# When the mixer runs: fixed stretches in place of a budget, and mirror blocks queued behind the last x

## The chip, the cores and the metric

The kernel runs on one core of one Trainium2 chip. The time is the device time of one execution in microseconds (us); the figure that counts is the median of the runs, and less is better.

## What is computed

For each of 8 batches there are 3008 rows of 256 channels (u, v) and of 64 channels (z). An attention without softmax gives x, and a token and channel mixer follows:

```python
scores = (1 / S) * (z @ z.T)
x = u * ((np.maximum(scores, 0.0) ** 2) @ v)
h = np.maximum(x.T @ w_tok1, 0.0) @ w_tok2        # over rows: 3008 -> 256 -> 3008
y = x + h.T
out = y + np.maximum(y @ w_ch1, 0.0) @ w_ch2      # over channels: 256 -> 1536 -> 256
```

## The kernel before, in words

**Tiles.** The rows of a batch make 6 column blocks q of 512 (the last has 448) and 6 key groups g of 512. Block (b, q) is the sum over all g of attention(g, q) times v(g), held transposed in two PSUM pairs, acc0 and acc1, one for each half of the channels. A score matmul (L424) contracts over 64 rows and uses half of TensorE's rows, and so does the attention product acc (L646), which is split into two 64-row halves. The two halves of a pair run side by side: this text calls that half mode. All products of the mixer use all 128 rows: full mode. Going from one to the other is a mode switch; the planner counts 0.095 us for it (`on_pe`).

**From scores to attention.** Each score pair goes through a relu on ScalarE (`relu`, L462; L450 for the diagonal) and a square on VectorE (`square`, L470; `square_triangle`, L499) into a buffer `at` (6 of them). The scores are symmetric, so block (b, q) for g > q is computed once and turned for block (b, g): `flip` (L515) issues a DMA transpose on SyncE's queue from `at` into a buffer `fl` (10 of them). These turned ones are the mirror blocks. The diagonal block ("triangle", q = g, from batch 2 on) is computed for its upper part alone, and three small DMA transposes in place (`flip_tiles`, L511) fill in the lower part before the product reads it.

**End of a block.** `finish` adds the two halves of acc (ScalarE copy L771, VectorE add L777), `gate` (L798) multiplies with the turned u and writes xT, and `turn_x` (L811) turns x by a DMA transpose on SyncE's queue.

**Mixer of a batch** (`add_mixer`). Two lists of pieces: heads are 6 token products `tok1` (L851, into a_ps), which need the last x of the batch, then 6 `tok2` (L870, into h_ps), whose result is added to xT; tails are for each block 6 channel products `ch1` (L911, into hp, relu on ScalarE L925 or VectorE L927 into h2pre) and 3 or 4 output tiles `ch2` (L955, into op), whose residual add (L971) needs another turned copy of xT (L893) and ends in a store (L976). One such list is worked off in its own order.

**Order of the work.** The order on every engine is fixed when the program is built, by a planner with its own costs. PSUM is a ring of bank pairs that scores, acc and mixer share. The main loop (from L1260) picks at each step a score unit, an attention step or a mixer piece. The mixer was let in by a budget: every attention or score step of batch 1 and later adds to it in proportion to its time, every mixer piece draws on it, and a stretch may begin only between blocks, from batch 1 on, before an even q. Loads (u, v, z) are software DMAs on GpSimd's queue, asked for at fixed steps of the block loop (`at_group`) and issued at least 4.5 us apart (`ask_some`), each behind a small copy (`mark`, L120) that ties it to finished work. SyncE's queue takes all transposes and all stores in program order, so an instruction that waits there holds up all behind it.

Of the kernel before, what the change touches and what calls it, by code (L numbers as in the profile page):

```python
# [44 lines left out]
class Piece:  # L45


    def __init__(self, cost, needs, fn, opens=False, closes=False, room=None,
                 urgent=False):
        self.cost, self.needs, self.fn = cost, needs, fn  # L50
        self.opens, self.closes, self.room = opens, closes, room
        self.urgent = urgent


@with_exitstack
def kernel(
# [12 lines left out]
    B, S, D = u.shape  # L69
# [398 lines left out]
    def square(unit, view, t):  # L468
        (b, q, g), pr = unit
        nc.vector.tensor_mul(view, view, view)  # L470
        if (b, q, g) in early:
            for e in early[b, q, g][2 * pr:2 * pr + 2]:
                e.t = t
            if pr == 0:
                blocks[b, q, g] = (
                    Done(t), ats[b, q, g].rearrange("p (i w) -> p i w", w=QW), "at", [1])
            else:
                ats.pop((b, q, g))
            return
        if pr < GK // 2 - 1:  # L480
            return
        at = ats.pop((b, q, g))
        uses = [1]
        if flips(b, q, g):
            uses[0] = 2
            attn = at.rearrange("p (j i s) -> p i j s", i=GK, s=P)
            done = push("sp", t, 1.8, 6.5, lambda t: flip(b, q, g, at, uses, done),
                        room=("fl",))
        else:
            attn = at.rearrange("p (i w) -> p i w", w=QW)  # L490
        blocks[b, q, g] = (Done(t), attn, "at", uses)
        recent[0] = at[:, :1]
# [212 lines left out]
    def do_half(start, g):  # L705
        blk = cur[0]
        if blk.whole:
            return do_whole(start, g)
        if blk.g is None:
            start_bundle(blk, g, start)  # L710
        g, dh, tiles = blk.steps[blk.half]
        blk.half += 1
        final = blk.slot == NG and not any(
            d == dh or d is None for _, d, _ in blk.steps[blk.half:])
        if dh is not None and blk.acc[dh] is None:
            blk.home[dh], free_at = take_slot()
            blk.acc[dh] = bank_pair(blk.home[dh], f"acc{dh}")
            start = max(start, free_at)
        start, end = on_pe(start, "half", len(tiles) * column_time(blk.W))
        for i in tiles:  # L720
            for h in range(2):
                av_matmul(blk, g, i, h if dh is None else dh, h, final and i == tiles[-1])
        if final:
            finish(blk, dh, end)
        if blk.half == len(blk.steps):
            blk.g = None
            for g in blk.bundle:
                _, _, name, uses = blocks.pop((blk.b, blk.q, g))
                release(name, uses, pe[0] + 0.2)
                used[blk.b, g] = used.get((blk.b, g), 0) + 1  # L730
                if blk.b == 0 and blk.q == NQ - 1:
                    live["fl"] -= 1
            if blk.slot == NG:
                end_block(blk)
# [52 lines left out]
    def gate(blk, dh, acc, t):  # L787
        b, q, W = blk.b, blk.q, blk.W
        uT = uTs[b, q]
        if dh == 0:  # L790
            xTs[b, q] = sb.tile([P, DT, QW], BF16, tag="xT", name="xT", bufs=ROOM["xT"])
            live["xT"] += 1
            live["x"] += 1
            if W < QW:
                nc.gpsimd.memset(xTs[b, q][:, :, W:], 0.0)
        xT = xTs[b, q]
        full, rest = W // P, W % P
        nc.vector.tensor_mul(  # L798
            xT[:, dh, :full * P].rearrange("p (t s) -> p t s", s=P),
            acc[:, :full * P].rearrange("p (t s) -> p t s", s=P),  # L800
            uT[:, :full, dh, :])
        if rest:
            nc.vector.tensor_mul(
                xT[:, dh, full * P:W], acc[:, full * P:W], uT[:, full, dh, :rest])
        if dh == DT - 1:
            gated[0] += 1
            push("sp", t, 1.25, 7.5, lambda t: turn_x(b, q, t), first=1)

    def turn_x(b, q, t):
        x = sb.tile([P, DT, QW // P, P], BF16, tag="x", name="x_sb", bufs=ROOM["x"])  # L810
# [23 lines left out]
    def add_mixer(b):  # L834
# [163 lines left out]

        for q in range(NQ):
            heads.append(Piece(0.874, [x_done[b, NQ - 1]], lambda end, q=q: tok1(q, end),  # L1000
                               opens=q < NQ - 1, closes=q > 0))
        for q in range(NQ):
            heads.append(Piece(4 * column_time(widths[q]), [a_done, tok2_done[q]],
                               lambda end, q=q: tok2(q, end)))
        def add_ch1(q, c2):
            h2_done[q, c2] = Done()
            tails.append(Piece(4 * column_time(widths[q]), [u_done[q]] + w_done[:2],
                               lambda end: ch1(q, c2, end),
                               room=("h2", "us") if c2 == 0 else ("h2",)))

        def halves(q):

# [10 lines left out]
        def add_ch2(q, half, i):  # L1023
            two = not alone(q, half)
            needs = [Sooner(h2_done[q, c2], 0.218 * c2) for c2 in range(CHT // 2)]
            tails.append(Piece(1.312, needs + w_done[2:],
                               lambda end: ch2(q, half, i, end), opens=two and i == 0,
                               closes=two and i == 1))


        early = ROOM["h2"] - CHT // 2
        for q in range(NQ):
            for c2 in range(early if q else 0, CHT // 2):
                add_ch1(q, c2)
            if q + 1 < NQ:
                for c2 in range(early):
                    add_ch1(q + 1, c2)
            for half in halves(q):
                for i in range(pieces_of(q, half)):
                    add_ch2(q, half, i)  # L1040

    def next_piece(t):

# [8 lines left out]
        for l in lists:  # L1052
            if not l:
                continue
            p = l[0]
            if p.opens and not p.closes and opened[0] is not None:
                continue
            r = max(t, known(*p.needs))
            if p.room and not has_room(p.room):
                r = FAR  # L1060
            if not p.closes:
                r = max(r, min(slots)) if slots else FAR
            if r < FAR and r <= t + 0.05:
                return r, l
            if r < best[0]:
                best = r, l
# [77 lines left out]
    for b in range(B):  # L1144
# [9 lines left out]
        if b + 1 < B:  # L1154
            at_group(base + NG, lambda b=b: new_zT(b + 1))
            for j, c in enumerate(vorder):
# [2 lines left out]
                    if j % 3 == 2:  # L1159
                        at_group(base + NG + j // 3 + 8, lambda b=b, j=j: turn_next_z(b, j // 3))  # L1160
                else:
                    at_group(base + 2 * NG + 2 + j,
                             lambda b=b, j=j: ask(lambda: z_then_turn(b + 1, j)))
                    at_group(base + (NQ - 1) * NG - 2 + (j if j > 1 else 0),
                             lambda b=b, c=c, j=j: ask(
# [61 lines left out]
    for k, item in enumerate(items):  # L1227
        at_group(NG + 1 + k * (NQ * NG - 2 * NG + W_LATER) // len(items), item)

    per_batch = 0.87 * NQ * (2 + CHT // 2) + 1.35 * 4 * NQ  # L1230
    flat = NQ * NG * 1.73 + NQ * (NQ + 1) / 2 * 0.44
    fill(7, bank_pair(0, "wp")[:, 0, :])

    for c in range(DT):
# [12 lines left out]
    late_z(5, 9.0)  # L1247
    first_u(18.5)

    done_units = 2  # L1250
    budget = 8.0
    NOW = 0.05
    STARVED = 0.7
    BACKLOG = 0.9
    GRAIN = 2
    SWING = 2.0
    SPACING = 4.5
    SLOW = 0.84
    LONG = 12.0
    while cur[0] is not None or heads or tails:  # L1260
        run_engines(pe[0])
        ask_some()
        t = pe[0]
        ta, g = next_half(t)
        tm, pieces = next_piece(t)
        blk = cur[0]

        def has_turned(us):
            return known(*(turned[b, c] for (b, q, g_), _ in us for c in (q, g_)))
# [30 lines left out]
        by_then = [s for d, s in ring if (guess.get(s, FAR) if d.t is None else d.t) <= need]  # L1300
        spare = need > t + 1.7 or len(by_then) > 1

        between = blk is None or blk.acc[0] is None
        mixer_now = tm <= t + NOW and (budget > -SWING or blk is None)
        pick = None

        together = (
            runs and blk.q > 1 and not blk.tails
            and blk.slot == 0 and t + 0.3 < tails_ready(blk) < FAR)
        if not runs:  # L1310
            if mode[0] == "full" and mixer_now:
                pick = "mixer"
            elif mode[0] == "half" and between and mixer_now and (
                    blk is None or blk.b > 0 and blk.q % 2 == 0):
                pick = "mixer"
            elif n_now and spare and queued < BACKLOG and ts <= t + NOW:
                pick = "scores"
            elif ta <= t + NOW:
                pick = "av"
            elif n_now and spare and ts <= t + NOW:  # L1320
                pick = "scores"
            elif mixer_now:
                pick = "mixer"
        elif n_now and not together and ts <= t + NOW and (whole or (low and n_now >= 2)):
            pick = "scores"
        elif (starved and now and can_score(done_units, now) == now
# [8 lines left out]
        elif ta <= t + NOW:  # L1335
            pick = "av"
        if pick is None:
            options = [(ta, "av"), (tm, "mixer")]
            if n_now and (whole or low if runs else spare):
                options.append((ts, "scores"))  # L1340
            when, what = min(options)
            op = next_op()
# [22 lines left out]
                for f in fetch.get(s, []):  # L1365
                    f()
        else:
            if not pieces[0].urgent:
                budget -= pieces[0].cost
            do_piece(tm, pieces)  # L1370
        if pick != "mixer" and blk is not None and blk.b >= 1:
            budget += per_batch * (pe[0] - t) / flat * (SLOW if blk.b == 1 else 1.0)
    run_engines(FAR)


# [28 lines left out]
```

## Time and profile before

| What | Value |
|---|---|
| median of 5 runs (lowest to highest) | 1147.67 us (1146.7 to 1148.45) |
| the profiled execution: its time, its span | 1148.45 us, 1146.7 us |
| TensorE matmuls | 9219 |
| VectorE, ScalarE, GpSimd busy | 56%, 48%, 13% |
| hardware DMA queue (transposes, stores), software DMA queue (loads): share of the 16 engines | 58.0%, 21.5% |

The span runs from the first to the last instruction. "L646" is line 646 of the kernel, "acc<-at,v_sb" reads: writes tile acc, reads tiles at and v_sb. SPq is SyncE's queue: the time shown there is that of issuing a DMA, and the landing is later. In a timeline equal instructions that follow each other are merged, with their count behind an x.

### The profile page before, as it was taken

To read this page: it belongs to the slowest core of one execution; us is meant where nothing else is said; L and a number is where in the kernel's file an instruction comes from. 1 tells how busy PE (TensorE), PEld (TensorE's weight loads), DVE (VectorE), ACT (ScalarE), POOL (GpSimd) and SP (SyncE) were. 2 spreads that over 40 slices of the span, in tenths; PEclk is the share of its full clock that TensorE was granted. 3 is DMA by queue.
4 is the path that set the end of the run, shared out by engine and by line. 5 is a ranking of instruction groups with operands and counts; after the bars stand their busy time and mean duration, and the time that the engine had idled before them with its cause. 6 is when DMAs were issued, how large, how long until landed. Compare 5 with 4: busy or idle time off the path is not lost.

```text
span 1146.7 us, 22470 instructions
## 1 busy us (share of the span) xinstructions
PE 1137.0 (99%) x9219; PEld 673.4 (59%) x9219; DVE 638.4 (56%) x947; ACT 549.3 (48%) x699; POOL 154.2 (13%) x387
## 2 busy tenths in 40 slices
PE   8999999999999999999999999999999999999998
PEld 3455465646557566565565655665566556566666
DVE  6887454565554755537545375554644656434544
ACT  7999534374342742526525354344543554422331
POOL 4500110200111001111111100111002110000000
PEclk9999999999999999999999999999999999999999
DMA  9999964985979868799588996799877998642121
GB/s 155 187 177 193 185 124 100 196 139 125 158 136 200 163 113 156 127 201 162 113 157 142 175 183 108 154 144 186 164 125 141 146 184 152 120 103 56 51 83 65
DMA packets 468199, 164.85 MB, mean 144 GB/s; under 512 B 431936, under 2 KB 445824, under 8 KB 468096
## 3 DMA queue, kind: packets, MB, share of 16 engines
q1 hardware_dynamic: 440240, 130.72, 58.0%
q0 software_dynamic: 27344, 32.32, 21.5%
q8 instruction: 72, 1.18, 0.4%
q10 hardware_dynamic: 512, 0.38, 0.1%
q14 instruction: 31, 0.25, 0.1%
HBM read 65.40 MB, written 24.64 MB: 79 GB/s over the span
## 4 chain that ended last, share of the span: by engine, by line
PE 97%; DMA 2%; DVE 0%; ACT 0%; SPq 0%; issue 0%; POOL 0%; ACTq 0%; DVEq 0%
PE acc L646 40%; PE op L955 21%; PE hp L911 21%; PE sc L424 6%; PE a_ps L851 4%; PE h_ps L870 4%; PE first_acc L563 1%; DMA zf<-in_z_dram 1%; DMA fl<-at 0%; DMA at<-at 0%; DMA v_sb<-in_v_dram 0%; DVE h2pre L927 0%; ACT at L462 0%; SPq L159 0%; PE up L1196 0%
## 5 line engine op out<-in xcount | busy, mean ns | idle before, releaser
L646 PEld LDWEIGHTS <-v_sb 64*128 64x128 bf16 x4418 | 239.5, 94 | 224.1 <-issue 6.5
L646 PE MATMUL acc<-at,v_sb 64*128 64x512 bf16 (+1 forms) x2738 | 341.8, 374 | 1.7 <-ACT at L462 1.3
L925 ACT ACTIVATE h2pre<-hp 128x1024 bf16<-128x1024 f32 (+1 forms) x161 | 160.8, 1000 | 315.0 <-PE hp L911 314.7
L462 ACT ACTIVATE at<-sc 128x1024 bf16<-128x1024 f32 (+1 forms) x294 | 288.0, 1027 | 33.8 <-PE sc L424 26.5
L911 PE MATMUL hp<-xT,w_ch_sb 128*128 128x512 bf16 (+1 forms) x1152 | 257.3, 375 | 0.0
L470 DVE TENSOR_TENSOR at<-at 128x1024 bf16<-128x1024 bf16 (+1 forms) x294 | 200.7, 687 | 100.8 <-ACT at L462 97.2
L955 PE MATMUL op<-w_ch_sb,h2pre 128*128 128x256 bf16 x2208 | 251.4, 273 | 0.3 <-DVE h2pre L927 0.2
L955 PEld LDWEIGHTS <-h2pre 128*128 128x128 bf16 x2208 | 215.4, 98 | 38.0 <-issue 2.2
L927 DVE TENSOR_SCALAR h2pre<-hp 128x1024 bf16<-128x1024 f32 (+1 forms) x127 | 153.8, 1211 | 91.5 <-PE hp L911 91.5
L646 PE MATMUL acc<-fl,v_sb 64*128 64x512 bf16 (+1 forms) x1680 | 195.0, 367 | 0.0
L911 PEld LDWEIGHTS <-w_ch_sb 128*128 128x128 bf16 x1152 | 111.8, 98 | 125.7 <-issue 4.4
L971 DVE TENSOR_TENSOR res<-op,u_sb 128x512 f32<-128x512 f32 x87 | 60.2, 691 | 153.4 <-PE op L955 153.3
L424 PE MATMUL sc<-zT 64*128 64x512 bf16 (+1 forms) x732 | 132.2, 360 | 0.2 <-ACT zT L1237 0.2
L777 DVE TENSOR_TENSOR cp<-acc,cp 128x512 f32<-128x512 f32 (+1 forms) x94 | 63.4, 675 | 101.4 <-ACT cp L771 100.6
L771 ACT COPY cp<-acc 128x512 f32<-128x512 f32 (+1 forms) x89 | 51.5, 578 | 131.3 <-PE acc L646 116.3
L450 ACT ACTIVATE at<-sc 128x512 bf16<-128x512 f32 (+3 forms) x144 | 52.1, 440 | 54.4 <-PE sc L424 53.7
L424 PEld LDWEIGHTS <-zT 64*128 64x128 bf16 x732 | 40.3, 94 | 42.2 <-issue 6.9
L798 DVE TENSOR_TENSOR xT<-cp,uT 128x512 bf16<-128x512 f32 (+1 forms) x94 | 62.4, 665 | 3.1 <-PE hp L911 1.4
L879 DVE TENSOR_TENSOR xT<-xT,h_ps 128x1024 bf16<-128x1024 bf16 (+1 forms) x48 | 55.7, 1173 | 9.5 <-PE h_ps L870 9.3
L120 POOL CAST mark<-at 128x1 f32<-128x1 bf16 x49 | 13.2, 269 | 341.8 <-DVE at L470 329.6
L499 DVE TENSOR_TENSOR at<-at 128x512 bf16<-128x512 bf16 (+3 forms) x144 | 38.1, 320 | 30.1 <-ACT at L450 24.9
L932 POOL COPY hs<-h2pre 128x128 bf16<-128x128 bf16 x48 | 15.7, 326 | 252.5 <-ACT h2pre L925 232.9
(56 smaller groups left out, 342.7 us busy)
## 6 DMA issues: line engine op xcount, KB each, us to landing
out_dram<-res SPq DMA_DIRECT2D x87, 256.0 KB, 2.3
v_sb<-in_v_dram POOLq DMA_DIRECT2D x40, 256.0 KB, 6.1
ur<-in_u_dram POOLq DMA_DIRECT2D x40, 256.0 KB, 5.7
w_tok_sb<-in_moe_w_tok_dram POOLq DMA_DIRECT2D x10, 256.0 KB, 9.5
zs<-in_z_dram POOLq DMA_DIRECT2D x35, 64.0 KB, 3.5
at<-at SPq DMA_TRANSPOSE x108, 2.5
fl<-at SPq DMA_TRANSPOSE x105, 5.5
v_sb<-in_v_dram POOLq DMA_DIRECT2D x8, 192.0 KB, 4.5
```

The lines of the kernel that those rows point to most:

```text
L424: nc.tensor.matmul(sc[:, r, c0:c1], zT[h, k:k + P], zT[h, m + c0:m + c1], start=True, stop=True)
L462: nc.scalar.activation(view, sv, ACT.Relu, scale=inv_S)
L470: nc.vector.tensor_mul(view, view, view)
L646: nc.tensor.matmul(o, vs[blk.b, g][rows, i, dh * P:(dh + 1) * P], rhs, start=(dh, h) not in blk.begun, stop=stop, skip_group_check=True)
L777: nc.vector.tensor_add(cp[:, :W], acc[:, 0, :W], cp[:, :W])
L798: nc.vector.tensor_mul(xT[:, dh, :full * P].rearrange("p (t s) -> p t s", s=P), acc[:, :full * P].rearrange("p (t s) -> p t s", s=P), uT[: ...
L879: nc.vector.tensor_add(to, to, h[:, :, :n * P].rearrange("p h (s t) -> p h t s", t=n))
L911: nc.tensor.matmul(hp[:, r, :W], w_ch1_sb[:, dc, cc * P:(cc + 1) * P], xT[:, dc, :W], start=(dc == 0), stop=(dc == DT - 1))
L925: nc.scalar.activation(h2[:, :, :W], hp[:, :, :W], ACT.Relu)
L927: nc.vector.tensor_single_scalar(h2[:, :, :W], hp[:, :, :W], 0.0, AX.max)
L955: nc.tensor.matmul(op[:, i, :], h2, w_ch2_sb[:, cc, :], start=(cc == 0 and (i == 0 or apart)), stop=(cc == CHT - 1), skip_group_check=True)
L971: nc.vector.tensor_add(res.rearrange("p i (h d) -> p i h d", d=P), op.rearrange("p i (h d) -> p i h d", d=P), us[:, :, half * 2:half * 2 + ...
```

## The change

Each mixer piece now carries a key: (batch, 0) for `tok1`, (batch, 1) for `tok2`, (batch, 2 + block) for `ch1` and `ch2`. A piece may run only when its key is not above the goal. The goal rises at the start of fixed blocks: at (b, 0) to (b-1, 1), which lets in what is left of batch b-2 (the channel products of its blocks 3, 4, 5) and all token products of batch b-1; at (b, 3) to (b-1, 4), which lets in the channel products of blocks 0, 1, 2 of batch b-1. While pieces up to the goal are left, the loop picks nothing but the mixer. Batch 1 has goals of its own at blocks 2 and 3. So attention runs in threes of blocks, with one mixer stretch after each three; the budget is gone.

A mirror block of batch 2 or later now goes to SyncE's queue only after the last x of the batch before it has gone there. The planner takes 12.0 instead of 7.5 us for the turning of that last x. The z loads for the next batch are asked for one block earlier. A two-row-group step of the last key tile no longer counts as the end of a half of the channels.

```diff
@@ __init__ of Piece
-                 urgent=False):
+                 urgent=False, key=(0, 0)):
@@ square
-                        room=("fl",))
+                        room=lambda: has_room(("fl",)) and (
+                            b < 2 or x_done[b - 1, NQ - 1].t is not None))
@@ do_half
-        final = blk.slot == NG and not any(
+        final = dh is not None and blk.slot == NG and not any(
@@ gate
-            push("sp", t, 1.25, 7.5, lambda t: turn_x(b, q, t), first=1)
+            push("sp", t, 1.25, 7.5 if q < NQ - 1 else 12.0, lambda t: turn_x(b, q, t), first=1)
@@ next_piece
             p = l[0]
+            if not p.urgent and p.key > goal[0]:
+                continue
@@ the loads of z
-                    at_group(base + 2 * NG + 2 + j,
+                    at_group(base + NG + 2 + j,
@@ the main loop
-    budget = 8.0
+    FIRST, EARLY, LATE = 4, 1, 4
+    goals = {(1, 2): (0, 0), (1, 3): (0, FIRST)}
+    for b in range(2, B):
+        goals[b, 0] = (b - 1, EARLY)
+        goals[b, NQ // 2] = (b - 1, LATE)
...
+        if blk is None:
+            goal[0] = (B, 0)
+        elif blk.acc[0] is None:
+            goal[0] = max(goal[0], goals.get((blk.b, blk.q), (-1, 0)))
         tm, pieces = next_piece(t)
-        blk = cur[0]
+        mixing = any(l and l[0].key <= goal[0] for l in (heads, tails))
...
-        mixer_now = tm <= t + NOW and (budget > -SWING or blk is None)
...
-            if mode[0] == "full" and mixer_now:
-                pick = "mixer"
-            elif mode[0] == "half" and between and mixer_now and (
-                    blk is None or blk.b > 0 and blk.q % 2 == 0):
-                pick = "mixer"
+            if mixing:
+                pick = "mixer" if tm <= t + NOW else None
...
-            options = [(ta, "av"), (tm, "mixer")]
-            if n_now and (whole or low if runs else spare):
+            options = [(tm, "mixer")] if mixing and not runs else [(ta, "av"), (tm, "mixer")]
+            if not mixing and n_now and (whole or low if runs else spare):
...
-            if not pieces[0].urgent:
-                budget -= pieces[0].cost
             do_piece(tm, pieces)
-        if pick != "mixer" and blk is not None and blk.b >= 1:
-            budget += per_batch * (pe[0] - t) / flat * (SLOW if blk.b == 1 else 1.0)
```

More of the change, by code (lines that the diff above doesn't have):

```diff
@@ L48, in __init__ @@
     def __init__(self, cost, needs, fn, opens=False, closes=False, room=None,
-                 urgent=False):
+                 urgent=False, key=(0, 0)):
         self.cost, self.needs, self.fn = cost, needs, fn
         self.opens, self.closes, self.room = opens, closes, room
-        self.urgent = urgent
+        self.urgent, self.key = urgent, key
 @with_exitstack
@@ L1000, in add_mixer, with add_ch1 @@
             heads.append(Piece(0.874, [x_done[b, NQ - 1]], lambda end, q=q: tok1(q, end),
-                               opens=q < NQ - 1, closes=q > 0))
+                               opens=q < NQ - 1, closes=q > 0, key=(b, 0)))
         for q in range(NQ):
             heads.append(Piece(4 * column_time(widths[q]), [a_done, tok2_done[q]],
-                               lambda end, q=q: tok2(q, end)))
-        def add_ch1(q, c2):
+                               lambda end, q=q: tok2(q, end), key=(b, 1)))
+        def add_ch1(q, c2, by):
             h2_done[q, c2] = Done()
@@ L1008, in add_ch1 @@
                                lambda end: ch1(q, c2, end),
-                               room=("h2", "us") if c2 == 0 else ("h2",)))
+                               room=("h2", "us") if c2 == 0 else ("h2",),
+                               key=(b, 2 + by)))
         def halves(q):
@@ L1027, in add_ch2 @@
                                lambda end: ch2(q, half, i, end), opens=two and i == 0,
-                               closes=two and i == 1))
+                               closes=two and i == 1, key=(b, 2 + q)))
         early = ROOM["h2"] - CHT // 2
@@ L1033, in add_mixer @@
             for c2 in range(early if q else 0, CHT // 2):
-                add_ch1(q, c2)
+                add_ch1(q, c2, q)
             if q + 1 < NQ:
                 for c2 in range(early):
-                    add_ch1(q + 1, c2)
+                    add_ch1(q + 1, c2, q)
             for half in halves(q):
@@ L1040, in add_mixer @@
                     add_ch2(q, half, i)
+    goal = [(-1, 0)]
     def next_piece(t):
@@ L1228 @@
         at_group(NG + 1 + k * (NQ * NG - 2 * NG + W_LATER) // len(items), item)
-    per_batch = 0.87 * NQ * (2 + CHT // 2) + 1.35 * 4 * NQ
-    flat = NQ * NG * 1.73 + NQ * (NQ + 1) / 2 * 0.44
     fill(7, bank_pair(0, "wp")[:, 0, :])
@@ L1255 @@
     GRAIN = 2
-    SWING = 2.0
     SPACING = 4.5
-    SLOW = 0.84
-    LONG = 12.0
     while cur[0] is not None or heads or tails:
@@ L1264 @@
         ta, g = next_half(t)
+        blk = cur[0]
+        if blk is None:
+            goal[0] = (B, 0)
+        elif blk.acc[0] is None:
+            goal[0] = max(goal[0], goals.get((blk.b, blk.q), (-1, 0)))
         tm, pieces = next_piece(t)
-        blk = cur[0]
+        mixing = any(l and l[0].key <= goal[0] for l in (heads, tails))
         def has_turned(us):
@@ L1301 @@
         spare = need > t + 1.7 or len(by_then) > 1
-        between = blk is None or blk.acc[0] is None
-        mixer_now = tm <= t + NOW and (budget > -SWING or blk is None)
         pick = None
@@ L1321 @@
                 pick = "scores"
-            elif mixer_now:
-                pick = "mixer"
         elif n_now and not together and ts <= t + NOW and (whole or (low and n_now >= 2)):
```

## The prediction

> **What bounds the kernel now.** I read the page first, for the engine without idle time:
>
> ```profile
> PE 1137.0 (99%) x9219; PEld 673.4 (59%) x9219; DVE 638.4 (56%) x947; ACT 549.3 (48%) x699; POOL 154.2 (13%) x387
> ...
> PEclk9999999999999999999999999999999999999999
> ...
> PE 97%; DMA 2%; DVE 0%; ACT 0%; SPq 0%; issue 0%; POOL 0%; ACTq 0%; DVEq 0%
> ```
>
> TensorE is busy for 99% at the full clock and makes 97% of the chain that ended last. The built order of the changed kernel has the same 9219 matmuls, so only what stands between matmuls can change. I went through the matmul starts in order of time and compared each distance with the streaming time (512 columns: 376 ns shown, but one pair of halves every 0.215 us). Streaming makes 1109.7 us of the 1146.7; 1.2 lie before the first matmul and 4.9 after the last one's start; some 17 are about 2.6 ns for each issue. What is left is some 3.7 us of start-up, 6.3 us of mode switches, and 3.8 us of stalls behind the start-up. Only the last two can be won.
>
> **Mode switches.** The timeline of TensorE around two of them:
>
> ```profile
> 506.29 2.78 PE L955 MATMUL op<-w_ch_sb,h2pre 128*128 128x256 bf16 x24
> 509.01 3.63 PE L646 MATMUL acc<-at,v_sb 64*128 64x512 bf16 x32
> ...
> 531.18 1.91 PE L646 MATMUL acc<-at,v_sb 64*128 64x512 bf16 x16
> 533.02 1.04 PE L870 MATMUL h_ps<-w_tok_sb,a_sb 128*128 128x512 bf16 x4
> ```
>
> 16 attention matmuls are 8 pairs, 8 x 0.2154 = 1.72 us, but the next product starts 1.84 us after the first: 0.11 us lost. The other way 24 x 0.109 = 2.62 us, and acc starts 2.72 us later: 0.10. Over all switches the trace gives 0.110 and 0.1055 us. Less the ordinary 2.6 ns that is 0.21 us for a pair of switches. In the built order there are 60 switches before and 46 after, 7 pairs fewer: 7 x 0.21 = **-1.5 us**. The Trainium skill ("TensorEngine Tiling (Array Packing)", Key Properties) says that a change of tiling mode drains TensorE, and "TensorE: Matmul & The Clock Gate" (Single matmul latency) puts the fixed part of one warm, isolated matmul at 166 ns; by it the estimate would be 14 x 0.166 = -2.3 us. The trace shows two thirds of that at every switch, so I use the trace. Nothing hides a switch, because TensorE is the bound.
>
> **Stalls that go.** The longest is in batch 1:
>
> ```profile
> 131.91 1.03 PE L646 MATMUL acc<-fl,v_sb 64*128 64x512 bf16 x8
> 134.29 1.04 PE L646 MATMUL acc<-at,v_sb 64*128 64x512 bf16 x8 [1.35 <-ACT at L462]
> ```
>
> and ScalarE's in the same stretch:
>
> ```profile
> 133.32 1.73 ACT L462 ACTIVATE at<-sc 128x896 bf16<-128x896 f32 x2 [1.86 <-DMA fl<-at]
> ```
>
> A relu waits until a flip has read the buffer it wants, and acc waits for the relu; the starts lie 2.38 us apart for 0.86 us of streaming, a stall of 1.5. In the changed order a mixer stretch of some 38 us begins just ahead of this place, and the score unit concerned comes after it: **-1.5**. A stall of 0.47 us at 990.2 waits for a triangle's transposes in block (7, 3). That block now follows a stretch, and its triangle has 43 us between scores and use: **-0.5**. Ten waits of 0.03 to 0.17 us stand where a stretch and a block meet (S to acc 281.50, 420.60, 560.18 and so on): PSUM pairs came back only 1.1 to 1.25 us of TensorE work after their last write. In the changed order I counted this distance for every pair in steady state: no such boundary is left below 1.9 us. **-0.9**. In the last stretch one output tile stalled 0.33 us on a relu with 1.1 to 1.6 us of cover (1076.4); it has 1.85 now: **-0.3**. What is late next at all these places is nothing within 1 us, by the same count. Together -3.2.
>
> **Costs that come.** (1) In the first stretch one hp finds its PSUM pair only 0.86 us after the last write, and the relu behind it takes 0.2 + 1.02 us: **+0.4**, once. (2) Blocks (b, 0), (b, 1), (b, 2) now run without a mixer between (b, 1) and (b, 2). The triangle of (b, 2) had 33 us between its last score and its first use; it has 13.8 now. Its transposes stand late in SyncE's queue:
>
> ```profile
> 517.81 6.12 SPq L518 DMA_TRANSPOSE fl<-at  x3
> 524.02 1.32 SPq L228 DMA_TRANSPOSE uT<-ur  x1
> 525.44 3.92 SPq L811 DMA_TRANSPOSE x_sb<-xT  x1
> 529.46 3.34 SPq L518 DMA_TRANSPOSE fl<-at  x1
> 532.90 3.76 SPq L511 DMA_TRANSPOSE at<-at  x3
> ```
>
> SyncE's order and TensorE's order from the start of (b, 0) to these three are the same in both kernels, so their landing carries over. In batch 4, (b, 0) starts at 509.0 and the third transpose lands at 537.8, 28.8 us later. The changed kernel uses it 30.1 us after the start (29.5 to the block, three pairs more to the fourth key tile). So 1.3 us are left; for batches 2 to 7 the same sum leaves 0.8, 2.9, 1.3, 1.7, 0.9 and 0.2 us. Those with a z to load (2 to 6) get something new: the z loads asked for one block earlier now start some 21 and 25 us after the block's start, just where this queue is full. How much they delay it no row shows. From below it is nothing (or a gain: the five flips of (b, 0) no longer run up to this block's start). From above: in the trace a u load of 256 KB issued at 524.11 lies over the uT at 524.02, which lands after 8.3 us against a median of 4.8, 3.5 later; two z loads have 64 KB each, so half, 1.7. The Trainium skill ("DMA: Bandwidth & Descriptors", Queues, rings and completion order) says that each DMA engine takes turns between the queues it has work for, packet by packet. By that rule two z loads in flight for 3.5 us each (the page's median landing) would halve the transposes' rate for 7 us, a delay of 3.5, and five batches would stall 2.7 + 0.6 + 2.2 + 1.8 + 2.6 = 9.9 us. The row of the u load is nearer, and z1 overlaps only the end: I take 1.2, a stall of 0.4 + 0.3 = **+0.7** (0 to 2.1 by the trace). (3) Places that the counts do not see, twelve new boundaries at some 0.04 us: **+0.5** (0 to 1).
>
> **What is moved at no cost.** The five flips of (b, 0) now stand in SyncE's queue behind x of (b-1, 5) and one more transpose. Behind them wait stores and the u copies of the residual adds. Five flips issue in some 2.0 us each and land after 5.5, while the stretch in front of (b, 0) has 39 us and the first mirror use comes 73 us after its scores; without that cover the last of them would land some 16 us after x, and blocks would wait for it. The buffers `at` stay full meanwhile, but no scores are made during a stretch. Token products wait for the last x with three blocks of channel products before them: 15 us between block end and the first tok1, against 2.2 us of adding and gating and a median landing of 4.0. The channel products of three blocks are already waiting, so if x came 5 us late the order would still have tok1 stand first, and TensorE would wait for it; I see no reason for that. ScalarE in the window of 24 us from 509 is busy for 18.2 (76%); a third block adds 8 units x 1.03 + 2 x 0.58 = 9.4 us in 11.7, so it stays below full. Weights for batch 0's token products, needed 12 us earlier than before, landed by 86.8.
>
> **Sum.** -1.5 - 3.2 + 0.4 + 0.7 + 0.5 = **-3.1 us**. The profiled execution has 1148.45 us, 1.75 outside its span, and is the slowest of the five runs; nothing in the sum touches that part, so I put the difference on the median: 1147.67 - 3.1 = **1144.6 us**. A measurement can tell about 0.2%, 2.3 us, from no change: below 1145.4 is faster, above 1150.0 slower.
>
> **The rivals.**
> - **All clean:** costs (2) and (3) are nothing: -1.5 - 3.2 + 0.4 = -4.3, 1143.4 us. For it: every distance that I could count grew. Against: the margins of 0.2 to 0.9.
> - **Only the switches:** stalls come back at other places, as waits for DMA did in batch 1 once already: -1.5, or 1146.2 us, no change that can be told. For it: the small stalls are of a kind that a planner moves as easily as it removes.
> - **SyncE's queue binds at the triangle of (b, 2), slower:** if its transposes land later by d than before, the stall is the sum of d less the margins. It eats all the rest of the gain (3.8) at d = 1.75 us, and passes +2.3 us at d = 2.2. With d = 2.5 in all six batches it is 1.7 + 0 + 1.2 + 0.8 + 1.6 + 2.3 = 7.6, thus 1151.5 us. For it: one uT was late by 3.5, and the queue is busy without a gap from 517 to 540. Against: no z is loaded in batch 7, and a z load is a quarter of a u load.
>
> **How the numbers follow.** Forecast 0.43 (1143.9 to 1146), all clean 0.20, only the switches 0.22, SyncE's queue 0.15. Below 1145.4 lie all of the clean case and most of the forecast: faster 0.60. The rest of the forecast and the switches case make 0.27 same; slower 0.13. The range goes from the sum without any cost of (1) to (3), 1147.67 - 4.7 = 1143.0, with 0.2 for the scatter of the runs, 1142.8, up to 1148.8, which takes in the switches case and the mild end of the queue case.
>
> **What would show it.** Right: 46 switches of 0.11 and 0.10; no wait of over 1 us behind 110 us; TensorE's row shows acc followed by acc between (b, 1) and (b, 2). Wrong: a wait of acc on "DMA at<-at" some 30 us after each (b, 0) starts, with SyncE's transposes later than 29 us; a wait of tok1 on "DMA x_sb<-xT"; or waits of hp on ScalarE early in a stretch.

## The result, and the profile after

The changed kernel takes 1152.56 us in the median (43 runs), the kernel before 1147.45 us (80 runs). The ratio is 1.0042, 95% interval 1.0031 to 1.0053: slower by 0.42%, 5.1 us in the medians. The forecast had 1144.6 and faster; the time lies above the range. The profiled execution takes 1152.39 us with a span of 1150.6, against 1146.7 before: 3.9 us more. One run of the changed kernel (1166.9 us, at a mean granted clock of 0.993) and two of r1_control were in a slower state of the chip and are left out of all times here.

The page of the changed kernel, the rows that answer to the first three shown of before:

```profile
PE 1137.4 (99%) x9219; PEld 663.4 (58%) x9219; DVE 638.2 (55%) x944; ACT 554.4 (48%) x702; POOL 149.4 (13%) x387
...
PEclk9999999999999999999999999999999999999999
...
PE 94%; DMA 3%; ACT 1%; issue 1%; DVE 0%; SPq 0%; ACTq 0%; POOL 0%
```

The first two rows are as good as unchanged, and neither would warn anyone. The chain does: TensorE fell from 97% to 94%, a DMA has 3%. The row of lines below it names that DMA: fl<-at, a flip, with 3% against 0% before.

TensorE's timeline at the first stretch and at a switch (start, duration, and how many equal matmuls were merged):

```profile
133.83 1.03 PE L912 MATMUL hp<-xT,w_ch_sb 128*128 128x512 bf16 x4
134.99 1.02 PE L871 MATMUL h_ps<-w_tok_sb,a_sb 128*128 128x512 bf16 x4
135.97 1.02 PE L912 MATMUL hp<-xT,w_ch_sb 128*128 128x512 bf16 x4
...
515.82 4.09 PE L956 MATMUL op<-w_ch_sb,h2pre 128*128 128x256 bf16 x36
519.84 1.47 PE L647 MATMUL acc<-at,v_sb 64*128 64x512 bf16 x12
```

Where acc once stalled for 1.5 us, a stretch runs. Four hp are 0.86 us, but the next start is 1.16 later, then 0.98 for 0.86: 0.30 + 0.12 us, the "+0.4, once" of the prediction. At the switch 36 x 0.109 = 3.92 us and acc follows 4.02 after the first: 0.10. There are 46 switches.

SyncE's queue in batch 4, around the transposes of the triangle of (4, 2):

```profile
543.36 4.71 SPq L512 DMA_TRANSPOSE at<-at  x3
```

The run of three blocks starts at 519.84, so the three are issued by 28.2 us after it; the last lands at 29.4, and acc, which needs it 30.1 us after the start, does not stall. In batch 6, whose run starts at 800.04, it does:

```profile
825.53 3.77 SPq L512 DMA_TRANSPOSE at<-at  x3
```

The third of these lands at 830.44, and the acc that reads it starts at 830.48, 0.22 us late. That is all that came of the cost which the prediction put there.

What came besides is in the list of waits (engine and line, what it waited for, then us in total, times, longest). Before:

```profile
ACT at L462 <- DMA fl<-at: 2.7, 2, 1.9
```

and after:

```profile
ACT at L462 <- DMA fl<-at: 26.1, 17, 4.5
...
ACT at L450 <- DMA fl<-at: 4.4, 3, 4.0
```

ScalarE waits for flips to have read the buffers `at`. Not all of it reaches TensorE. Compared with its streaming time and the usual cost of a switch, TensorE has these further stalls, all in the last scores of (b, 2) or at the first hp of the stretch behind it: batch 3, 1.17 and 0.17 us; batch 4, 0.41 and 0.34; batch 6, 1.49 and 0.17; batch 7, 3.45 and 0.15. With the 0.22 at the triangle they make 7.6 us. Batches 2 and 5 have none. The worst, batch 7, in the timelines of the changed kernel. SyncE's queue:

```profile
958.83 3.44 SPq L812 DMA_TRANSPOSE x_sb<-xT  x1
962.36 2.67 SPq L519 DMA_TRANSPOSE fl<-at  x1
965.12 4.16 SPq L512 DMA_TRANSPOSE at<-at  x3
969.38 7.39 SPq L519 DMA_TRANSPOSE fl<-at  x2
```

GpSimd, which asks for the loads:

```profile
971.19 0.53 POOL L218 DMA_DIRECT2D ur<-in_u_dram  x1 [0.32 <-issue]
```

ScalarE and TensorE:

```profile
979.30 0.98 ACT L450 ACTIVATE at<-sc 128x512 bf16<-128x512 f32 x2 [4.02 <-DMA fl<-at]
```

```profile
976.02 1.04 PE L647 MATMUL acc<-fl,v_sb 64*128 64x512 bf16 x8
980.33 0.39 PE L424 MATMUL sc<-zT 64*128 64x512 bf16 x2 [3.27 <-ACT at L450]
...
981.66 4.69 PE L912 MATMUL hp<-xT,w_ch_sb 128*128 128x512 bf16 x14
```

Read them from the bottom up. The score at 980.33 waits for a PSUM pair that the relu of the next triangle (L450) has to empty. That relu waits 4.02 us for a flip. The two flips of 969.38 take 7.39 us to issue. The first takes 1.7; the second starts at 971.14, takes 5.62, and lands at 979.20. At 971.19, beside its start, GpSimd issues a load of u of 256 KB; another had gone out at 957.39. The bill goes on after the stall, as the stretches by time show (length, busy us of PE, PEld, DVE, ACT, POOL, then granted clock, DMA share and GB/s):

```profile
977.00:985.00 8.00, 4.73 (x21) 1.73 (x19) 4.26 (x9) 4.33 (x8) 1.46 (x4) 0.79 0.93 201
```

The granted clock is 0.5 from 981.32 to 984.73, and the first eight hp take 1.50 us longer together (0.21 us each, the last 0.05). This is of the profiled execution.

### The profile page after: what moved, and what is told of

Its sections match the earlier page's. It is cut to its first block, busy times and chain, and to the rows that moved or that the text cites. A ratio compares the mean times of both kernels' runs of the same rounds, so it can differ in the third digit from the quotient of the medians.

```text
span 1150.6 us, 22510 instructions
## 1 busy us (share of the span) xinstructions
PE 1137.4 (99%) x9219; PEld 663.4 (58%) x9219; DVE 638.2 (55%) x944; ACT 554.4 (48%) x702; POOL 149.4 (13%) x387
## 4 chain that ended last, share of the span: by engine, by line
PE 94%; DMA 3%; ACT 1%; issue 1%; DVE 0%; SPq 0%; ACTq 0%; POOL 0%
PE acc L647 38%; PE hp L912 21%; PE op L956 21%; PE sc L424 6%; PE a_ps L852 4%; PE h_ps L871 3%; DMA fl<-at 3%; PE first_acc L564 1%; ACT at L462 1%; DMA zf<-in_z_dram 1%; DMA v_sb<-in_v_dram 0%; ACT at L450 0%; DVE xT L880 0%; ACT cp L772 0%; DVE xT L799 0%
## 5 line engine op out<-in xcount | busy, mean ns | idle before, releaser
L647 PEld LDWEIGHTS <-v_sb 64*128 64x128 bf16 x4418 | 228.3, 94 | 229.7 <-issue 2.3
L462 ACT ACTIVATE at<-sc 128x1024 bf16<-128x1024 f32 (+1 forms) x294 | 290.0, 1024 | 139.3 <-PE sc L424 96.9
L926 ACT ACTIVATE h2pre<-hp 128x1024 bf16<-128x1024 f32 (+1 forms) x164 | 163.3, 999 | 297.7 <-PE hp L912 297.3
L928 DVE TENSOR_SCALAR h2pre<-hp 128x1024 bf16<-128x1024 f32 (+1 forms) x124 | 150.5, 1213 | 106.7 <-PE hp L912 106.3
L647 PE MATMUL acc<-fl,v_sb 64*128 64x512 bf16 (+1 forms) x1680 | 191.0, 367 | 0.0
L450 ACT ACTIVATE at<-sc 128x512 bf16<-128x512 f32 (+3 forms) x144 | 52.5, 442 | 61.7 <-PE sc L424 56.7
L778 DVE TENSOR_TENSOR cp<-acc,cp 128x512 f32<-128x512 f32 (+1 forms) x94 | 63.4, 675 | 28.9 <-ACT cp L772 28.2
L871 PE MATMUL h_ps<-w_tok_sb,a_sb 128*128 128x512 bf16 (+1 forms) x192 | 47.9, 375 | 0.1
```

The source lines that it names most:

```text
L462: nc.scalar.activation(view, sv, ACT.Relu, scale=inv_S)
L647: nc.tensor.matmul(o, vs[blk.b, g][rows, i, dh * P:(dh + 1) * P], rhs, start=(dh, h) not in blk.begun, stop=stop, skip_group_check=True)
L778: nc.vector.tensor_add(cp[:, :W], acc[:, 0, :W], cp[:, :W])
L871: nc.tensor.matmul(h[:, dh, :W], st["a"][:, th, dh * P:(dh + 1) * P], w_tok2_sb[:, th, q * QW:q * QW + W], start=(th == 0), stop=(th == 1))
L926: nc.scalar.activation(h2[:, :, :W], hp[:, :, :W], ACT.Relu)
L928: nc.vector.tensor_single_scalar(h2[:, :, :W], hp[:, :, :W], 0.0, AX.max)
```

## The experiments

Two sums are used as a ruler. From the first acc of (b, 0) to that of (b, 3), summed over batches 2 to 7, the changed kernel takes 422.5 us; and its ScalarE waits 26.1 us at L462 for flips.

### First: is it a lack of buffers?

To give `fl` or `at` one more buffer, something had to give way, so there is a control with less elsewhere. Control, then one more `fl`, then one more `at`; the fourth takes one `fl` from the changed kernel as it is.

```diff
@@ r1_control; r2_fl11 has "fl": 11 besides, r3_at7 "at": 7
-    ROOM = {"at": 6, "fl": 10, "xT": 9, "x": 7, "h2": 8, "us": 2}
+    ROOM = {"at": 6, "fl": 10, "xT": 9, "x": 6, "h2": 8, "us": 2}
@@ load_u: ur
-bufs=3
+bufs=2
@@ the landing of z: zf
-bufs=7
+bufs=6
@@ r4_fl9, from the changed kernel
+    ROOM = {"at": 6, "fl": 9, "xT": 9, "x": 7, "h2": 8, "us": 2}
```

The control:

> The changed kernel with one x buffer less (6 for 7) and one u buffer less (2 for 3), to make room for the next two runs; 6 buffers at and 10 buffers fl as before. Theory FL: in the run of blocks (b,0) to (b,2) the mirror blocks want 11 buffers fl at once, 10 are there, so a flip on SyncE's queue waits until TensorE has read one, its buffer at stays taken, a relu waits, TensorE stalls at the end of (b,2). Rival DMA: the transposes are only too slow in that run. Rival AT: the buffers at are too few. All three expect what the changed kernel has: ratio to before 1.003 to 1.005, stalls of acc and sc of 0.4 to 3.5 us at the end of (b,2) in several batches.

It took 1163.68 us, ratio 1.0114 (1.0060 to 1.0168), more than any of the three expected. The control is not neutral: with fewer buffers SyncE's queue waits once for 11.7 us for a load of u early on, and (1, 3) starts at 184.9 us against 169.1. From batch 2 on it has stalls at the places of the changed kernel's, 3.66 us in batch 7, so its trace can serve as a basis there; its time cannot.

> The control with 11 buffers fl for 10, nothing else. Theory FL: the stalls at the end of (b,2) go (some 9 us in the profiled execution), no flip waits for TensorE for over 2 us there; 1143 to 1145 us, ratio to before 0.996 to 0.998. Rival DMA: no change, ratio 1.003 to 1.005. Rival AT: gain under 1 us.

It took 1162.79 us, 1.0116 (1.0076 to 1.0157), the same as its control. The stalls stay: 0.85, 0.29, 1.43 and 3.68 us. SyncE's queue and ScalarE in batch 7:

```profile
983.32 7.75 SPq L519 DMA_TRANSPOSE fl<-at  x2
```

```profile
993.27 0.98 ACT L450 ACTIVATE at<-sc 128x512 bf16<-128x512 f32 x2 [4.10 <-DMA fl<-at]
```

With eleven buffers the slow flip no longer waits for TensorE to release an `fl`. It takes 6.0 us to issue all the same, and lands 8.1 after that start, beside a load of u at 984.92. So it isn't a lack of `fl`; that theory falls.

> The control with 7 buffers at for 6, 10 buffers fl. Theory FL: flips still wait for TensorE as long as before in (b,2), but one more score block is in hand, so most of the stall is hidden: 1144 to 1149 us. Rival DMA: the same, but without waits of flips for TensorE. Rival AT: all stalls go, 1143 to 1144 us.

It took 1174.32 us, 1.0209 (1.0170 to 1.0248), worse than its control. One more `at` lets one more score pair through ahead of the stretch, and its relu then stands ahead of hp's relus on ScalarE. TensorE and ScalarE in batch 4:

```profile
580.76 7.46 PE L912 MATMUL hp<-xT,w_ch_sb 128*128 128x512 bf16 x26 [3.75 <-ACT at L462]
```

```profile
579.69 1.94 ACT L462 ACTIVATE at<-sc 128x1024 bf16<-128x1024 f32 x2 [5.17 <-DMA fl<-at]
```

The wait for a flip is as long as ever; it has moved into the stretch. The owners of `at` are late, and another buffer only changes who waits for them.

> The changed kernel with 9 buffers fl for 10. Theory FL: the flips meet the limit one block earlier and wait longer; 5 to 15 us more than the changed kernel, 1157 to 1167 us. Rivals DMA and AT: within 1 us of the changed kernel.

It took 1173.57 us, 1.0223 (1.0183 to 1.0264). That is more than even FL expected. New stalls of 2.0 to 3.7 us stand some 20 us into the run from (b, 3). Nine are too few at another place; that says nothing on the end of (b, 2).

### Second: the loads, the mirror blocks' wait, the length of the run

```diff
@@ r5_u_late: the u asked for in blocks 1 and 2; r9: q in (1,); r10: q in (2,)
-                    at_group(base + q * NG + 2, lambda m=m: ask(lambda: u_then_turn(m)))
+                    at_group(base + (2 * NG + 5 if b > 1 and q in (1, 2) else q * NG + 2),
+                             lambda m=m: ask(lambda: u_then_turn(m)))
@@ r6_uz_late: r5, and z as late
-                    at_group(base + NG + 2 + j,
+                    at_group(base + (2 * NG + 5 if b > 1 else NG + 2 + j),
@@ r7_no_mirror_wait; r12_u_late_no_mirror is r5 with this
-                        room=lambda: has_room(("fl",)) and (
-                            b < 2 or x_done[b - 1, NQ - 1].t is not None))
+                        room=("fl",))
@@ r8_pairs
-        goals[b, NQ // 2] = (b - 1, LATE)
+        goals[b, 2] = (b - 1, 3)
+        goals[b, 4] = (b - 1, 5)
@@ r11_z_back
-                    at_group(base + NG + 2 + j,
+                    at_group(base + 2 * NG + 2 + j,
```

> The changed kernel, but from batch 2 on the u loads that were asked for in blocks (b,1) and (b,2) are asked for at the end of (b,2), so that they run beside the mixer stretch. Theory LOAD: a flip that SyncE issues while a u load is in flight takes 3 to 6 us to issue instead of 1.7 and lands later, so its buffer at comes late, a relu waits and TensorE stalls at the end of (b,2); without the u load there the flips issue in about 1.7 to 2.3 us and the stalls of 0.4 to 3.5 us at the end of (b,2) go: 1143 to 1146 us, ratio 0.996 to 0.999. Rival QUEUE: SyncE's queue is simply too full in a run of three blocks, whatever else loads: stalls stay, ratio 1.003 to 1.005.

It took 1144.71 us, 0.9974 (0.9964 to 0.9983): faster than both kernels. Between 135 and 1132 us no stall is longer than 0.16 us, TensorE makes 99% of the chain, and ScalarE's wait is back at 2.8 us.

> The same, and the z loads too are asked for at the end of (b,2). Theory LOAD: at most 1 us better than with the u loads alone, since a z load holds a flip up by well under 1 us: 1143 to 1146 us. Rival QUEUE: 1.003 to 1.005.

It took 1145.67 us, 0.9985 (0.9978 to 0.9992). Postponing z as well gains nothing; three stalls of 0.5 to 1.5 us come in the run from (b, 3).

> The changed kernel without the wait of mirror blocks for the last x. Theory LOAD: the five flips of (b,0) lie in another place, long before the stall; nothing at the end of (b,2) changes: ratio 1.003 to 1.005. Rival MIRROR: the wait pushes the flips together and is the cost: back to 1.000 or under.

It took 1152.99 us, 1.0052 (1.0039 to 1.0065), with the stalls of the changed kernel (1.60, 0.98, 1.47, 3.11 us and smaller ones). The wait of the mirror blocks isn't the cause.

> The changed kernel with three stretches for each batch, one after every two blocks, of fixed contents: two blocks of channel products each, the first with all token products. Theory LOAD: as in the kernel before, the scores of (b,2) are done before the second stretch, which hides their flips, so no stall at the end of a run over 0.5 us; six pairs of switches more than the changed kernel, +1.3 us: 1144.5 to 1147.5 us. Rival QUEUE: the same. Rival STRETCH (fixed contents with token products in one piece cost time in themselves): 1150 us and over.

It took 1147.32 us, 0.9999 (0.9981 to 1.0016). With a stretch after every second block, all else as changed, the stalls at (b, 2) are gone; so is the saving, with 58 switches and a stall of 0.33 us at an output tile in most batches.

> The changed kernel, with only the u load of block (b,1) moved to the end of (b,2), from batch 2 on. In batches 2 to 6 this is the only u load that lies in the run's second half, since that of (b,2) stands behind six z loads and comes only in the stretch; in batch 7, without z, both lie there. Theory LOAD: the stalls of batches 3 to 6 (some 4 us in all) go, that of batch 7 (some 5) goes in part or stays: 1145 to 1149 us, ratio 0.998 to 1.001. Rival QUEUE: 1.003 to 1.005.

It took 1144.37 us, 0.9970 (0.9954 to 0.9986), without stalls, batch 7 included, where LOAD had expected a part to stay. SyncE's queue in that batch:

```profile
963.98 9.14 SPq L519 DMA_TRANSPOSE fl<-at  x3
```

The load that was not moved comes at 967.95, 29.0 us after the start of (7, 0), as the second one does in the changed kernel (28.9). The flip beside it, the last of the three, takes 5.27 us to issue. But the two flips ahead of it are out by then, and nobody waits for this one. So a slow flip is not yet a stall, and in this order the second load alone does not make one; in batches 2 to 6 the first load is the only one that falls into the run, apart from one at its very start.

> The changed kernel, with only the u load of block (b,2) moved to its end. Theory LOAD: batches 2 to 6 keep their stalls (0 to 2 us each), since that load came after the run already; batch 7 loses part of its 5 us: 1147 to 1151 us, ratio 1.000 to 1.003. Rival QUEUE: 1.003 to 1.005.

It took 1153.17 us, 1.0052 (1.0031 to 1.0073). But the edit didn't move what it was to move. GpSimd in batch 7:

```profile
967.69 0.53 POOL L218 DMA_DIRECT2D ur<-in_u_dram  x1
981.48 0.53 POOL L218 DMA_DIRECT2D ur<-in_u_dram  x1 [0.33 <-issue]
```

Both loads come 10.3 us later than in the changed kernel (957.39 and 971.19), as everything there does: the stall stands at 990.50 in place of 980.33. TensorE's order is the same to the last matmul. This run only repeats the changed kernel, and neither its expectation nor a theory is tested by it.

> Both u loads late (the run that was fastest so far), and no wait of mirror blocks for the last x. Theory LOAD: without stalls at the end of (b,2) the mirror wait shows by itself: within 1.5 us of the run with both u loads late, 1143.5 to 1146 us. Should x come late for the token products without it, they would wait and the time would go up by 1 to 5 us.

It took 1144.82 us, 0.9983 (0.9961 to 1.0006): no difference from r5_u_late that can be told, though batch 6 has stalls of 0.41 and 0.94 us in the run.

> The changed kernel with the z loads asked for where they were before the change, one block later. Theory LOAD: the z loads no longer stand ahead of the u load of (b,2), so this one too is issued beside the flips in every batch, as in batch 7 of the changed kernel: each batch stalls like that one, 3 to 5 us, 1160 to 1175 us, ratio 1.010 to 1.024. Rival Z (the z loads are what holds the flips up, as the prediction had it): back to 1145 to 1148 us.

It took 1187.66 us, 1.0341 (1.0294 to 1.0389), far more than any theory gave. SyncE's queue and GpSimd in batch 2:

```profile
241.11 10.54 SPq L519 DMA_TRANSPOSE fl<-at  x3
```

```profile
242.77 0.53 POOL L218 DMA_DIRECT2D ur<-in_u_dram  x1 [0.32 <-issue]
```

With z at its old place no z stands ahead of the loads of u, and three of them now start within each run, the one shown being the first. But z is also turned later, so the scores of the next (b, 0) come later and more flips fall into the run. The two were not separated. This much follows: asking for z one block earlier, a part of the change, helps it. The planner's 12.0 us and the edit to the end of a half were not taken out by themselves.

### Third: the transfer, or the order?

r5 and r9 don't settle the cause. The planner counts loads, so it also put scores elsewhere (298 lines of difference in the 18438 of TensorE's order) and moved a turn of u. The last pair holds the order fixed on TensorE, ScalarE, VectorE and SyncE. The first of the two makes loads smaller; the second adds a load, with its mark, on GpSimd.

```diff
@@ r13_u_small, from the changed kernel: load_u, turn_u
+        if b > 1 and q in (3, 4):
+            nc.gpsimd.dma_start(out=ur[:, :1, :64], in_=rows_of(u[b], q)[:, :1, :64])
+        else:
+            nc.gpsimd.dma_start(out=ur[:, :n, :], in_=rows_of(u[b], q))
...
+        src = w_tok1_sb[:, :4, :] if b > 1 and q in (3, 4) else ur
@@ r14_u_extra, from r5_u_late
+    dead = consts.tile([P, 704], BF16)
+    def more_u(b, q):
+        after(recent[0])
+        nc.gpsimd.dma_start(out=dead[:], in_=rows_of(u[b], q).rearrange("p t d -> p (t d)")[:, :704])
...
+                    if b > 1 and q in (1, 2):
+                        at_group(base + q * NG + 2, lambda m=m: more_u(m // NQ, m % NQ))
```

> The changed kernel with the same order on every engine, but in batches 2 to 7 the u of blocks 3 and 4, which is loaded during the three-block run, is a load of 16 KB instead of 256 KB, and SyncE turns a part of the weights of the same size in its place; the u of these blocks is left out of the computation. The late loads (u_late, u_first_late) also let the planner put scores and one turn elsewhere, so they do not separate the load from the order. LOAD (the transfer itself holds the flip): the waits of ScalarE on fl<-at at the ends of (b,2) go, the stall of 3.4 us in batch 7 and the one half-clock stretch go: 1144 to 1147 us. ORDER (what matters is where scores and the turn stand in the queues): the stalls stay, 1150 to 1154 us.

It took 1143.53 us, 0.9969 (0.9952 to 0.9985). No stall is left at the end of (b, 2). From (b, 0) to (b, 3) the six batches take 413.5 us, 9.0 less than in the changed kernel: its 7.6 us of stalls and 1.5 of slow clock. The same place in batch 7 (line numbers here are 4 higher), SyncE's queue, GpSimd and TensorE:

```profile
954.57 1.26 SPq L816 DMA_TRANSPOSE x_sb<-xT  x1
955.92 1.69 SPq L523 DMA_TRANSPOSE fl<-at  x1
961.94 3.60 SPq L523 DMA_TRANSPOSE fl<-at  x2
```

```profile
966.81 0.53 POOL L219 DMA_DIRECT2D ur<-in_u_dram  x1 [0.33 <-issue]
```

```profile
972.73 1.04 PE L651 MATMUL acc<-at,v_sb 64*128 64x512 bf16 x8
973.70 4.49 PE L916 MATMUL hp<-xT,w_ch_sb 128*128 128x512 bf16 x19
```

The same two flips issue in 3.60 us, not 7.39, and hp follows acc 0.97 us later, 0.11 of it the switch. Both loads have a part in this. (7, 0) starts at 937.92 here and at 942.29 in the changed kernel, so SyncE comes to the two flips 24.0 us after the start against 27.1: beside the first load, now small, the turn of x takes 1.26 us and not 3.44, and the flip 1.69 and not 2.67. Both flips are out before the second load, 28.9 us after the start in both kernels. The changed kernel's second flip was late, met that load, and was issued only by 34.5. It cannot have waited for TensorE to release its `fl` until then: the order is the same, TensorE had not stalled before, and here the same flip is out by 27.6.

LOAD had ScalarE's waits gone. They are not:

```profile
ACT at L466 <- DMA fl<-at: 14.6, 13, 2.7
```

They are shorter, 2.7 us at most against 4.5, and that TensorE's queued work covers.

> The u_late kernel, same order on every engine, with a further load of 176 KB of u into a tile that nobody reads, issued behind a mark at the places where the changed kernel asks for the u of blocks 3 and 4 in batches 2 to 7. LOAD: flips at the end of (b,2) become slow again, and the stalls come back at least in part: 1147 to 1153 us. ORDER: with scores and turn where u_late has them, a load beside the flips costs little: 1144 to 1146 us.

It took 1169.10 us, 1.0183 (1.0160 to 1.0207): the direction that LOAD gave, far more than its 1147 to 1153. Stalls of 0.5 to 3.6 us are back in all six batches, in four of them with half a clock behind. SyncE's queue and TensorE in batch 4 (lines 7 higher):

```profile
556.59 5.96 SPq L526 DMA_TRANSPOSE fl<-at  x2
```

```profile
558.60 1.04 PE L654 MATMUL acc<-at,v_sb 64*128 64x512 bf16 x8
563.07 0.58 PE L431 MATMUL sc<-zT 64*128 64x512 bf16 x2 [3.42 <-ACT at L469]
```

A load that nobody reads makes the stalls, and in this batch not by lying over the slow flip. Of the two flips shown the second takes 3.86 us; both extra loads of this batch have landed by then, and what lies beside it is a load of z (557.77). In r5_u_late the same two flips take 3.55 us and start 25.4 us after (4, 0), here 29.0: the extra loads have made the queue late. They come on top of those already there and are not held back behind the z loads, which is probably why they cost more; that wasn't measured apart.

## Why the prediction was wrong

**Right.** The changed kernel without one kind of transfer takes 1143.5 us (r13_u_small), with it merely later 1144.7 (r5_u_late); the forecast was 1144.6, and its rival without costs (2) and (3), 1143.4. The other terms of the sum hold one by one: 46 switches at 0.10 to 0.11; the stalls of 1.5 and 0.47 us and that of the last stretch gone; of the ten small ones only six of 0.046 us left; +0.42 in the first stretch where +0.4 stood.

**Wrong size, no harm.** Cost (2), +0.7 for the triangle of (b, 2): 0.22 us, in batch 6, where the working had 0.3; the 0.4 of batch 2 did not come. The z loads that it feared lie in the same place in r13_u_small, where no stall is left.

**The step that failed** is the count that stands behind "no such boundary is left below 1.9 us" and "What is late next at all these places is nothing within 1 us, by the same count", with their companion in the part on moved work: "The buffers `at` stay full meanwhile, but no scores are made during a stretch." The count took the distance of TensorE's work for each PSUM pair. It did not follow the pair one step further, to the relu that empties it, to the buffer `at` that the relu needs, and to the flip that owns that buffer. The second sentence weighed the flips ahead of (b, 0), which a stretch covers. At the end of (b, 2) scores are made, with a run's flips behind them and no stretch to cover those; r8_pairs shows that a run of two blocks has no such stall. In the sum this belongs to cost (3), the places that the counts do not see, put at +0.5: it came to nearly 9.0 us (422.5 less 413.5, of which 0.22 belongs to the triangle), three times the whole gain. It also had two parts that a count of waits alone would miss: the long issue, and the slow clock afterwards.

**The rival** "SyncE's queue binds at the triangle of (b, 2)" gave 1151.5 at d = 2.5, close to 1152.56, and it had the right queue. That the number is close is luck, though. The place was the flips behind the triangle, which itself cost 0.22 us, and the loads whose bytes had to go were those of u. What a z load adds once the queue is late is open: no run took the bytes of z away and left u as it was. Its argument against itself was the wrong way round. "No z is loaded in batch 7" was to make that batch safe; it is the worst. With no z ahead of it the second u load comes 28.9 us after the start of (7, 0), among flips that the first has made late, while in batches 2 to 6 it stands behind six z loads. It seems to take both: r9_u_first_late has the second load at the same place, and no stall. The row that would have told was quoted in the prediction itself: a uT that landed 3.5 us late beside a u load. It was used to price z by its size. Even the long issue of a flip was to be seen in the trace of before, SyncE's queue and GpSimd in batch 7:

```profile
980.13 4.59 SPq L518 DMA_TRANSPOSE fl<-at  x1
```

```profile
979.93 0.53 POOL L218 DMA_DIRECT2D ur<-in_u_dram  x1 [0.35 <-issue]
```

There ScalarE still had free buffers, and no relu waited for it. But the stall of 0.47 us that the prediction booked as a gain comes right behind it. TensorE:

```profile
990.87 2.33 PE L646 MATMUL acc<-at,v_sb 64*128 64x512 bf16 x20 [0.31 <-DMA at<-at]
```

Behind the flip SyncE issues the triangle's transposes of (7, 3). The second takes 2.09 us, beside the next load of u at 986.71, and lands at 990.83; that is what acc waits for. So one stall of this kind was on the list already; how much of it the loads made was not tested. What would be worth knowing ahead of a change is not which waits are long but which have cover that the change takes away.

## What to carry to other kernels

When a change makes a stretch of work longer, follow each buffer round its whole circle: who frees it, behind which queue, and which cover that freeing had. Then look for the large transfers that fall into the stretch, and ask for them where their neighbours have slack; here that turned 0.4% slower into 0.3% faster, with the planner's order moved a little too. And an edit that moves a load also moves a planner's order: to blame the load, keep the order and change its bytes.

## What the runs showed of the hardware

**A load of 256 KB in flight lengthens the issue of a transpose, not only its landing.** In the changed kernel behind 200 us a flip takes 1.73 us to issue on SyncE in the median with no load in flight (23 flips), 2.31 beside a z load of 64 KB (19) and 2.63 beside a u or v load of 256 KB (48); the longest are 3.6, 3.98 and 6.97. Some of this may be a wait of the flip's own. In r13_u_small, with the same order, the medians are 1.76, 1.72 and 2.95 us (29, 19 and 42 flips): a z load by itself shows no effect there, and the two flips of batch 7 take 3.60 in place of 7.39 us. The Trainium skill's rule that a DMA engine takes turns between its queues ("DMA: Bandwidth & Descriptors", Queues, rings and completion order), used in the prediction for the landing of one transpose, leaves out that all behind it in SyncE's queue start later too; no trace here shows the turns themselves.

**A gap of TensorE can cost more than itself.** Behind the stall of 3.45 us the records show half the clock for 3.41 us; behind one of 3.9 us in r3_at7 and one of 2.35 us in r14_u_extra, too. The stall of 1.49 us in batch 6 shows none, nor one of 1.99 us in r14_u_extra. But the length of a gap doesn't settle it. r2_fl11 has 3.68 us at 994.30, the same place in batch 7, and the granted clock is 1.00 from 985 to 1000; r10_u_second_late has 3.3 us at 990.50, also at 1.00. The slow stretches last 3.41 or 6.83 us in these runs, once 10.24. When a gap brings one on wasn't tested by itself.
